# A new instruction order and another way of transposing half of the tiles, in a convolution and MLP kernel on one Trainium2 core

## The chip, the cores and the metric

The kernel runs on one core of a Trainium2 chip. The metric is device time in microseconds (us), lower is better. The core has five engines that run side by side, each in the order of its own queue: TensorE (PE: matmuls; its weight loads are listed as PEld), VectorE (DVE), ScalarE (ACT), GpSimd (POOL) and SyncE (SP, which here only issues DMAs). They wait for each other by semaphores. PE writes to PSUM, which DVE or ACT must empty ("evacuate") into SBUF. Sixteen DMA engines move data between HBM and SBUF, or within SBUF.

## The reference, cut to what matters

Sequence length S = 2048, width D = 640, hidden width F = 1728, all in bf16.

```python
x = A_q
# A: a gated long convolution
k_shift = 4-tap causal convolution of k, per channel (shift_k)
kv = k_shift * v
y  = irfft(rfft(kv, 2S) * rfft(ssm_k, 2S))[:S]      # convolution over the whole sequence
y  = y + kv * ssm_D
h  = x + layernorm(x) * y
# B: an MLP
a   = layernorm(h) @ w1 + b1
act = a * tanh(softplus(a))                          # Mish
h2  = h + act @ w2
```

## The kernel before, in words

The transform over the sequence is done by matmuls with tables, in stages. Channels go in five groups of 128, in three chunks (group 0; 1 and 2; 3 and 4). The names below are those of the operations in the order text; after the colon of each word there stands its engine (t PE, v DVE, a ACT, p POOL, d a DMA from SP).

- Loads: `d_n` (ssm_k), `d_k`, `d_v`, `d_g` (the table G), `d_x` (the input x in three parts).
- `k1pe` (line 543) transposes ssm_k on PE, `k1ev` evacuates, `dadd` (552) adds ssm_D to the first tap, so that the term kv * ssm_D needs no work of its own.
- `s1kpe`, `s1vpe` (469, 470): first stage of the forward transform of k and of kv, 20 groups each, of 16 weight loads and 16 matmuls. `ev` (374 on ACT, 376 on DVE) empties each group's PSUM bank, 1024 columns.
- `ktpe` (499), `ktsh` (508), `kspe` (522, 523): transposes of k and the 4-tap convolution; `kv` (528) multiplies by v on DVE.
- `s2kpe` (576), `s2vpe` (612): second stage with the table G. `s2kpe` needs every evacuation of `s1k`.
- `sw` (591, 592): DMAs that swap real and imaginary rows within SBUF. `p2` (631) and `p1` (628): the products of the two spectra, on DVE and POOL.
- `i1pe` (663, 664), then `i2pa`, `i2pb`, `i2pc` (734): the inverse transform; the last gives, for each of 16 tiles of 128 positions, a [128, 640] block y in PSUM. `d_t2m` loads its table; `d_w1` and `d_w2` load the MLP's weights.
- For each tile t: `y` evacuates, `lnx` (721, 723) is layernorm(x), `wb` (751; `wf`, 749, from PSUM for tiles 0 and 1) multiplies, `h` (755) adds x, `bn` and `pow` (760 to 765) take the statistics of h, `hc` (770) normalizes it into one of three buffers.
- `trpe` (778) transposes a normalized tile on PE, five blocks of 128x128, and `trev` (787) evacuates it into `lnhT`, where the tiles of a unit lie side by side: `lt_s` (315) has two buffers, in the memory of the table G, which is free by then.
- Units of 256, 256, 512, 512, 512 positions (tiles 0-1, 2-3, 4-7, 8-11, 12-15): `m1pe` (813, 809) is the product with w1, seven groups a unit; `hb` (822) applies bias and Mish on ACT; `m2pe` (839) is the product with w2, one a tile, 28 matmuls; `res` (849, 846) adds h and `d_out` (854, 861) stores. Tile 15 goes in three parts at the end.

PSUM is four buffers of 1024 columns, used in turn; PE can be at most four groups ahead of the evacuations.

The order of the work is written out: the text `ORDER` (from line 29 on) lists every operation with its engine. `_schedule` (143) walks it, gives each operation a start by the planner's costs, and picks the buffer of each ring that comes free first by those costs; the program is then emitted in the order of the starts. On each engine this is the order of the text; on SP, too. The planner has a rule for PE's instruction fetches (136, 161 to 169): instructions come in blocks, the next block is asked for as one is begun, it takes `_FETCH` 2.2 or, with transfers under way, `_SLOW` 5.0, and PE stands if it isn't there. [...]

## Time and profile before

| | |
|---|---|
| median of 3 runs | 233.67 us (232.84 to 280.52) |
| the profiled execution: time, span | 232.65 us, 230.9 us |
| instructions | 6501 |
| DMA traffic | 28.73 MB, mean 124 GB/s |
| granted TensorE clock, mean | 0.988 |
| ACT, evacuations L374 into uk (48) and uv (32) | 44.8 and 30.6 us |
| PE, second product L839 (462 matmuls) | 62.7 us |
| PE, first product L813 (318 records) | 57.9 us |

How to read it: the span is cut by windows (a stretch, then the busy time and, in brackets, the number of instructions of each engine, the clock that PE was granted, the share of the DMA engines and GB/s). The chain of work that ended last goes back from the last instruction to what released it; its rows give a start, a length and an engine with a line, and "issue" is time in which the engine waited for nothing that the profile shows. Groups give a line, an engine, an operation, what it wrote from what, the count, the busy time and the mean ns of one, and the idle time ahead of it. Lines are those of the kernel before.

### The profile page before, as it was taken

The page shows a single profiled execution, that of the slowest core. Times are in us where ns is not written, and L with a number is a line of the kernel's source. Part 1 is how long each engine was busy: PE and PEld are TensorE (multiplying, and loading weights), DVE is VectorE, ACT ScalarE, POOL GpSimd, SP SyncE. Part 2 cuts the span into 40 slices and gives each one's busy share as a digit, 9 for nine tenths or more (in the row PEclk, how much of TensorE's full clock was granted, in tenths as well). Part 3 has the DMA queues.
Part 4 walks back from the last instruction along what each step waited for, and adds up shares of the span by engine and source line. Part 5 has one row for each costly group of instructions (what it writes and reads, how often), then busy time and mean ns, then how long its engine had stood idle before and what let it go on. Part 6 is the DMA issues. An engine that isn't in the chain of part 4 may idle for free.

```text
span 230.9 us, 6501 instructions
## 1 busy us (share of the span) xinstructions
PE 219.5 (95%) x2842; PEld 169.1 (73%) x2849; DVE 139.2 (60%) x259; ACT 133.8 (58%) x184; POOL 70.7 (31%) x89
## 2 busy tenths in 40 slices
PE   7996999999789999999999999999999999999992
PEld 2986999899688999988877544777465445767772
DVE  0789899999997979888967735317921000112121
ACT  2576898999879999998827266311417608010000
POOL 0414850037770042764575891221000000000000
PEclk9999999999979999999999999999999999999998
DMA  6999992829962679500000100001100000001101
GB/s 189 420 382 398 429 404 76 231 61 282 317 161 82 230 285 385 166 0 4 0 3 0 57 1 3 0 28 60 57 0 31 0 0 0 31 0 57 61 28 57
DMA packets 19358, 28.73 MB, mean 124 GB/s; under 512 B 1409, under 2 KB 15746, under 8 KB 18946
## 3 DMA queue, kind: packets, MB, share of 16 engines
q1 hardware_dynamic: 19040, 28.17, 35.1%
q8 instruction: 22, 0.36, 0.6%
q10 hardware_dynamic: 194, 0.15, 0.2%
q14 instruction: 6, 0.05, 0.1%
q0 software_dynamic: 96, 0.00, 0.0%
HBM read 20.45 MB, written 2.62 MB: 100 GB/s over the span
## 4 chain that ended last, share of the span: by engine, by line
PE 79%; DVE 7%; ACT 7%; issue 4%; POOL 2%; DVEq 0%; ACTq 0%; POOLq 0%
PE ps L839 27%; PE ps L813 24%; ACT uv L374 4%; PE ps L734 4%; ACT uk L374 3%; PE ps L469 3%; PE ps L576 3%; PE ps L664 3%; PE ps L663 3%; PE ps L543 3%; PE ps L499 2%; PE ps L778 2%; PE ps L395 2%; DVE uv L376 2%; DVE ra L528 2%
## 5 line engine op out<-in xcount | busy, mean ns | idle before, releaser
L839 PE MATMUL ps<-rn,uv 128*128 128x320 bf16 (+2 forms) x462 | 62.7, 295 | 0.6 <-DVE xb L846 0.6
L822 ACT ACTIVATE uv<-ps,b1s 128x512 bf16<-128x512 f32 (+1 forms) x70 | 36.6, 605 | 42.1 <-PE ps L813 33.2
L813 PE MATMUL ps<-G 128*128 128x512 bf16 (+1 forms) x318 | 57.9, 336 | 0.4
L839 PEld LDWEIGHTS <-uv 128*128 128x128 bf16 x462 | 44.1, 98 | 17.0 <-issue 0.9
L813 PEld LDWEIGHTS <-G 128*128 128x128 bf16 x325 | 31.3, 98 | 23.4 <-issue 0.2
L374 ACT CAST uk<-ps 128x1024 bf16<-128x1024 f32 (+2 forms) x48 | 44.8, 1025 | 5.6 <-PE ps L470 3.4
L374 ACT CAST uv<-ps 128x1024 bf16<-128x1024 f32 x32 | 30.6, 1036 | 2.5 <-PE ps L470 2.0
L849 DVE TENSOR_TENSOR xb<-ps,xb 128x640 bf16<-128x640 f32 x5 | 4.1, 825 | 38.1 <-PE ps L839 38.1
L663 PE MATMUL ps<-a,uv 128*128 128x128 bf16 x160 | 18.5, 219 | 0.4 <-ACT uk L374 0.3
L663 PEld LDWEIGHTS <-uv 128*128 128x128 bf16 x160 | 17.9, 113 | 0.0
L376 DVE CAST uk<-ps 128x1024 bf16<-128x1024 f32 (+1 forms) x14 | 16.3, 1197 | 2.3 <-PE ps L664 1.2
L765 POOL TENSOR_TENSOR r<-ve,mhalf 128x1 f32<-128x1 f32 x16 | 9.1, 570 | 17.7 <-DVE ve L762 17.6
L612 PE MATMUL ps<-uv,G 128*128 128x64 bf16 (+1 forms) x384 | 13.7, 193 | 0.4 <-ACT uv L374 0.3
L612 PEld LDWEIGHTS <-G 128*128 128x128 bf16 x384 | 12.9, 101 | 1.0 <-issue 0.7
L374 ACT COPY G<-ps 128x640 bf16<-128x640 bf16 x8 | 5.5, 705 | 12.6 <-PE ps L778 12.6
L469 PE MATMUL ps<-cst,ra 128*64 128x128 bf16 x160 | 10.7, 220 | 2.2 <-issue 2.0
L528 DVE TENSOR_TENSOR ra<-ps,rb 128x1024 bf16<-128x1024 f32 x10 | 12.0, 1224 | 1.0 <-PE ps L523 1.0
L576 PE MATMUL ps<-uk,G 128*128 128x160 bf16 x128 | 11.7, 231 | 0.0
L469 PEld LDWEIGHTS <-ra 128*64 128x64 bf16 x160 | 9.3, 110 | 2.8 <-issue 2.4
L628 DVE TENSOR_TENSOR uv<-uv,uk 128x1024 bf16<-128x1024 bf16 x17 | 10.8, 686 | 0.1
L470 PE MATMUL ps<-cst,ra 128*64 128x128 bf16 x160 | 10.8, 221 | 0.0
L849 DVE TENSOR_TENSOR xa<-ps,xa 128x640 bf16<-128x640 f32 x6 | 4.9, 821 | 9.6 <-PE ps L839 9.6
(115 smaller groups left out, 377.0 us busy)
## 6 DMA issues: line engine op xcount, KB each, us to landing
G<-tab_g SPq DMA_DIRECT2D x8, 512.0 KB, 9.5
rn<-in_A_ssm_k_dram SPq DMA_DIRECT2D x5, 512.0 KB, 6.0
ra<-in_A_k_dram SPq DMA_DIRECT2D x4, 640.0 KB, 7.3
rb<-in_A_v_dram SPq DMA_DIRECT2D x2, 1280.0 KB, 12.4
G<-in_B_w_dram SPq DMA_DIRECT2D x5, 432.0 KB, 3.8
rn<-in_B_w_dram SPq DMA_DIRECT2D x1, 2080.0 KB
rn<-uk SPq DMA_DIRECT2D x4, 512.0 KB, 4.8
rb<-uk SPq DMA_DIRECT2D x4, 512.0 KB, 9.0
```

The lines of the kernel that those rows point to most:

```text
L374: nc.scalar.copy(o, i)
L376: nc.vector.tensor_copy(o, i)
L469: nc.tensor.matmul(ps[0:64, dgl, :], lhs, mc, start=True, stop=True)
L470: nc.tensor.matmul(ps[64:128, dgl, :], lhs, ms, start=True, stop=True)
L528: nc.vector.tensor_tensor(kv_w[:, m, :, 8 * h:8 * h + 8, :], rt.tile.rearrange("p (l t d) -> p d t l", l=4, t=8), raw_v[:, 8 * h:8 * h + 8 ...
L576: nc.tensor.matmul(ps[:, o:o + 160], g_v[:, f, :], KA[:, :, f, :], start=True, stop=True)
L612: nc.tensor.matmul(ps[:, fl * st:fl * st + n], g_v[:, f0 + fl, :], V[c.i][:, :, f0 + fl, :], start=True, stop=True)
L628: return eng.tensor_tensor(v, v, K[c.i][:, :, f0:f1, :], ALU.mult)
L663: nc.tensor.matmul(pz[:, dgl, :], V[c.i][:, dg // 4, :, dg % 4], a12[:, 0, :], start=True, stop=False)
L813: nc.tensor.matmul(ph[:, i * 512:i * 512 + w], w1[:, dc, fc * P:fc * P + P], lnhT_of(u)[:, dc, 0:w], start=(dc == 0), stop=(dc == NDC - 1))
L822: nc.scalar.activation(hb_of(u)[:, fc, 0:n], rt.tile[:, i * 512:i * 512 + n], ACT.Mish, bias=b1s[:, fc:fc + 1], scale=1.0)
L839: nc.tensor.matmul(po[:, a + a // 320 * 192:a + a // 320 * 192 + n], hb_of(u)[:, fc, o - x * w // 2:o - x * w // 2 + P], w2[:, fc + x, a:a ...
```

## The change

`MOVED = 3`: from unit 3 on, so for tiles 8 to 15, the normalized tile isn't transposed by PE. `hc` writes its 640 columns in another order (by 32 within each block of 128), a VectorE transpose (`dtr`) turns every 32x32 block of the tile, and DMAs within SBUF (`d_tr`, one for each pair of tiles, 16 DMAs of 32 partitions x 2 x 160 elements each, from SP's queue) carry the blocks to the partitions where they belong. The transposed pair lies in one of three new buffers in the memory of `uv0`, which the inverse transform has read by then. There are 40 transposes and 8 evacuations less, and 8 VectorE transposes and 64 DMAs more.

So that each DMA writes long rows, `lnhT` has another layout for all units: tile, then quarter of the tile (32 positions), then block of 128 channels, then position. `trev` of tiles 0 to 7 writes into it, and the first product reads its moving operand as 16 runs of 32 elements that are 160 elements apart.

And `ORDER` is a new text throughout; the planner and its rule for fetches are the same. On SP, `d_a12` goes from the head of the list to behind the `sw` of chunk 0, `d_x2` behind the first `sw` of chunk 2, and `sw0_1` and `sw1_1` stand next to each other; `d_small` (three small DMAs) stands earlier on POOL. Of `s2kev`, one of 22 is on DVE and 21 are on ACT (4 and 18 before). The two orders of PE in the first two stages:

```
before: ... k1pe3 s1kpe2_2 s1kpe2_0 s1kpe2_1 k1pe1 s1kpe2_3 s1kpe3_0 s1kpe0_1 s1kpe3_2 s1kpe3_3 s1kpe0_0 s1kpe1_3
  s1kpe0_3 k1pe4 s1kpe1_2 s1kpe1_1 s1kpe0_2 s1kpe4_0 s1kpe4_3 s1kpe4_2 s1kpe4_1 s1kpe3_1 s1kpe1_0 ktpe0_0 ...
  ... s1vpe3_0 s1vpe0_3 s1vpe3_1 s1vpe4_3 s1vpe4_0 s2vpe0_1 s1vpe4_1 s1vpe4_2 s1vpe3_3 s2vpe0_0 s2vpe2_7 ...
after:  ... k1pe1 s1kpe2_2 s1kpe2_3 s1kpe2_1 s1kpe2_0 k1pe4 s1kpe1_3 s1kpe0_1 s1kpe0_2 s1kpe1_1 k1pe3 s1kpe4_1
  s1kpe4_2 s1kpe0_0 s1kpe4_0 s1kpe1_0 s1kpe0_3 s1kpe3_1 s1kpe1_2 s1kpe3_0 s1kpe3_3 s1kpe3_2 s1kpe4_3 ktpe3_0 ...
  ... s1vpe4_1 s1vpe3_1 s1vpe3_3 s1vpe4_3 s1vpe0_1 s1vpe4_0 s1vpe3_0 s2vpe1_5 s2vpe0_1 s2vpe0_3 s2vpe2_6 ...
```

and of the second half:

```
after:  ... m2pe2 ... m1pe2_0 m2pe3 m2pe5 m2pe6 m1pe3_2 m2pe7 m1pe3_1 m1pe3_0 m1pe3_4 m1pe3_3 m1pe3_5 m1pe3_6 m2pe4 m2pe9 m2pe8
  m1pe4_1 m1pe4_6 m1pe4_5 m1pe4_4 m1pe4_2 m1pe4_0 m2pe11 m1pe4_3 m2pe10 m2ape15 m2pe13 m2pe12 m2pe14 m2bpe15 m2cpe15
DVE:    ... res5 res6 wb15 bn15 res7 hc14 dtr14 hc15 dtr15 res4 ...
SP:     ... d_w2 d_tr8 d_out1 d_out0 d_tr10 d_out2 d_out3 d_tr12 d_out5 d_out6 d_out7 d_tr14 d_out9 d_out4 ...
```

The diff outside of the order, cut:

```diff
+MOVED = 3
-    lt_s = [...rearrange("p (c s) -> p c s", c=NDC) for i in range(2)]
+    lt_s = [...rearrange("p (t r c j) -> p t r c j", t=4, r=4, c=NDC) for i in range(2)]
+    ht_s = [uv[0][:, i * 2 * D:(i + 1) * 2 * D].rearrange("p (t s) -> p t s", t=2) for i in range(3)]
...
             hc_rt.tile = slot(hc_rt, hc_s)
-            nc.vector.tensor_scalar(hc_rt.tile, xt(t2), mv2[:, t2, 0:1], r2[:, t2:t2 + 1], ALU.subtract, ALU.mult)
+            o, x = hc_rt.tile, xt(t2)
+            if U_OF[t2] >= MOVED:
+                o, x = o.rearrange("p (q c i) -> p c q i", q=4, i=32), x.rearrange("p (c q i) -> p c q i", q=4, i=32)
+            nc.vector.tensor_scalar(o, x, mv2[:, t2, 0:1], r2[:, t2:t2 + 1], ALU.subtract, ALU.mult)
...
+        if U_OF[t2] >= MOVED:
+            if t2 % 2 == 0:
+                ht_rt = _RT(R_HT)
+            def dtr(e, t2=t2, hc_rt=hc_rt, ht_rt=ht_rt):
...
+                nc.vector.transpose(ht_rt.tile[:, t2 % 2], hc_rt.tile)
...
+            def dmt(e, ht_rt=ht_rt, pair_of=pair_of):
+                dst = pair_of(2).rearrange("p t r c j -> p t r (c j)")
+                src = ht_rt.tile.rearrange("p t (q s) -> p t q s", q=4)
+                for r in range(4):
+                    for q in range(4):
+                        nc.sync.dma_start(dst[32 * q:32 * q + 32, :, r], src[32 * r:32 * r + 32, :, q])
...
-            ev(e, lnhT_of(u)[:, :, o:o + P], rtt.tile[:, 0:D].rearrange("p (c t) -> p c t", c=NDC))
+            ev(e, tile_of()[:, 0].rearrange("p r c j -> p c r j"), rtt.tile[:, 0:D].rearrange("p (c r j) -> p c r j", c=NDC, r=4))
...
-                        nc.tensor.matmul(ph[:, i * 512:i * 512 + w], w1[:, dc, fc * P:fc * P + P], lnhT_of(u)[:, dc, 0:w],
+                        nc.tensor.matmul(ph[:, i * 512:i * 512 + w], w1[:, dc, fc * P:fc * P + P], lnhT_of(u).rearrange("p t r c j -> p c (t r) j")[:, dc, 0:w // 32],
```

## The prediction

> **What bounds the kernel now.** I read the page's busy time first, then a table of windows, then the chain of work that ended last, and at the end single groups.

> ```profile
> PE 219.5 (95%) x2842; PEld 169.1 (73%) x2849; DVE 139.2 (60%) x259; ACT 133.8 (58%) x184; POOL 70.7 (31%) x89
> q8 instruction: 22, 0.36, 0.6%
> ```

> TensorE (PE) is busy for 95% of 230.9 us. The windows (length, then busy us and count on PE, PEld, DVE, ACT, POOL, then granted clock, DMA share, GB/s) show that this average covers two halves with different limits:

> ```profile
> 24.00:62.00 38.00, 37.65 (x855) 36.02 (x849) 35.96 (x38) 35.91 (x41) 15.98 (x15) 1.00 0.75 251
> ...
> 91.80:226.00 134.20, 133.62 (x1028) 90.29 (x1032) 59.64 (x149) 57.13 (x102) 37.75 (x45) 1.00 0.08 28
> ```

> From 91.8 to 226.0 PE lacks work for only 0.58 us, and VectorE (DVE), ScalarE (ACT) and the DMAs have much room. Whatever leaves PE there shortens the run by its own length, and nothing else can. From 24 to 62 three engines are full at once: PE 37.65, DVE 35.96, ACT 35.91 of 38. There an order of the same work can win only the little that all of them waste. The chain shows where PE stood for nothing that the profile names:

> ```profile
> 15.53 0.37 issue
> ...
> 21.59 1.06 issue
> ...
> 62.21 1.96 issue
> ```

> Beside them one wait that has a name, from the list of waits:

> ```profile
> PE ps L469 <- issue: 3.4, 3, 2.0
> ...
> PE ps L469 <- DVE rn L552: 0.8, 1, 0.8
> ```

> The same stretches as windows:

> ```profile
> 10.80:15.90 5.10, 4.68 (x130) 4.25 (x125) 4.80 (x5) 4.42 (x6) 1.33 (x3) 1.00 1.02 383
> 15.90:22.65 6.75, 4.88 (x130) 4.42 (x129) 5.84 (x8) 4.56 (x5) 2.23 (x2) 1.00 1.01 398
> 22.65:28.90 6.25, 6.25 (x129) 6.16 (x129) 5.29 (x9) 4.67 (x5) 5.50 (x5) 1.00 1.03 425
> 57.50:64.17 6.67, 4.54 (x146) 4.00 (x140) 6.61 (x8) 5.24 (x6) 4.75 (x4) 1.00 1.08 312
> 64.17:69.20 5.03, 4.87 (x126) 4.70 (x127) 5.03 (x9) 4.31 (x5) 3.74 (x6) 0.66 0.59 145
> ```

> Queue q8 moved 22 packets for 2842 + 2849 PE instructions, so one fetch brings about 259. Between the first two stalls PE ran 259 instructions, and in the window ahead of the third 286. I read the stalls as PE at the end of its block while the next is under way beside transfers (DMA share 1.01 and 1.08); a block then took 6.75 and 6.67 us. The third stall has a tail: from 64.17 to 69.20 the granted clock is 0.66, which loses 5.03 × 0.34 = 1.7 us.

> **The change, part by part.** All sums are against the profiled execution: span 230.9, time 232.65 us, so 1.75 lie around the span. The median of the three runs is 233.67, 0.4% above it.

> *PE's transposes of tiles 8 to 15 go.* They stand on the chain as pieces of L778:

> ```profile
> 148.42 0.56 PE ps L778 x10
> 148.98 3.80 PE ps L839 x28
> 152.78 0.28 PE ps L778 x5
> ...
> 156.87 0.28 PE ps L778 x5
> ...
> 167.67 0.56 PE ps L778 x10
> ...
> 174.19 0.28 PE ps L778 x5
> ...
> 176.63 0.28 PE ps L778 x5
> ```

> That is 40 transposes in 0.56 + 0.28 + 0.28 + 0.56 + 0.28 + 0.28 = 2.24 us, each with a product right behind it. I take **-2.24**. Their eight evacuations leave DVE and ACT (0.48 and 0.71 us each, next fence); off the path, nothing.

> *The first product reads its moving operand in runs of 32 columns.* The nearest rows are L576, whose moving operand is gathered in runs of 4, and L813 with its long rows:

> ```profile
> 27.29 0.42 PE ps L576 x6
> ...
> 129.53 10.74 PE ps L813 x49
> ```

> 0.42 / 6 / 160 = 0.44 ns per column against 10.74 / 49 / 512 = 0.43. Shorter runs cost PE nothing there, so I take 0.

> *Eight VectorE transposes, and a reordered hc.* No transpose on DVE is in this trace. The bounds for 128x640 are the plainest and the slowest rows of that size:

> ```profile
> L770 DVE TENSOR_SCALAR hc<-xb,mv,r 128x640 bf16<-128x640 bf16 x6 | 2.6, 440 | 0.0
> L376 DVE COPY G<-ps 128x640 bf16<-128x640 bf16 x8 | 3.9, 484 | 8.8 <-PE ps L778 8.5 <-ACT G L374 0.3
> L755 DVE TENSOR_TENSOR xa<-rb,xa 128x640 bf16<-128x640 bf16 x1 | 1.7, 1703 | 0.0
> L374 ACT COPY G<-ps 128x640 bf16<-128x640 bf16 x8 | 5.5, 705 | 12.6 <-PE ps L778 12.6
> ```

> So 0.44 to 1.70 us; I take 0.8, nearer the plain rows, as the operation also goes from SBUF to SBUF. Eight are 6.4 us (3.5 to 13.6), in a half where DVE is busy 59.64 of 134.20. Cost 0; the cover is the other work that PE has before units 3 and 4. hc at the 1.70 bound would add 10 us to DVE in the same room.

> *Sixty-four DMAs on SP's queue* (four pairs, 16 each), ahead of twelve of the result's DMAs. SP runs in order, and each DMA waits until the eighth before it has landed. SP's rows:

> ```profile
> L854 SPq DMA_DIRECT2D out_dram<-xa x6: 332/332/434, 157.8 to 224.3; - x6
> ...
> L591 SPq DMA_DIRECT2D xa<-uk x2: 1230/1232/1235, 39.7 to 50.9; - x2
> ...
> DMA to landing us min/median/max: 3.7/6.8/9.9
> ...
> DMA to landing us min/median/max: 1.8/1.8/2.7
> ...
> L849 DVE TENSOR_TENSOR xa<-ps,xa 128x640 bf16<-128x640 f32 x6 | 4.9, 821 | 9.6 <-PE ps L839 9.6
> ```

> The first landing line is L591's, the second L854's; the last row gives res7. One pair costs between 16 × 0.33 + 1.8 = 7.1 us and 16 × 1.23 + 9.9 = 29.6. I take about 12, nearer the low end, since these DMAs meet an idle fabric (share 0.08). Who waits: m1pe3 for pair 10, m1pe4 for pair 14. Pair 14 is tightest. After m2pe7 DVE does res7, two hc and two transposes, 0.82 + 0.88 + 1.6 = 3.3 us (2.6 to 5.1). Meanwhile PE has six groups of unit 3 (10 × 0.219 each, 13 us) and three second products (3.80 each, 11.4), so 24.4 in all. Pair 14 has 24.4 - 3.3 = 21 us, and needs 12: **0**. The results behind it on SP delay nobody; the last pair leaves over 50 us before the end.

> *The order of the first 92 us.* It moves what each engine waits for. In the new order, too, a block of PE instructions ends inside the k side's first stage, and another in the v side's, with sw2 and x2 on the queues. Each of these blocks is nearly all eight groups of 16 loads and 16 matmuls, 256 × 4.54 / 286 = 4.1 us of PE work by the fourth window. If a loaded fetch still takes 6.7 us, PE leaves those places when it did before. Bounds: all three stalls and the slow clock go, -(0.37 + 1.06 + 1.96 + 1.7) = -5.1; or the blocks stand for all that they are short of, 6.75 - 4.1 = 2.65 in place of 1.06 and of the 0.8 for L552's add, +0.8, and 6.67 - 4.1 = 2.6 in place of 1.96, +0.6. I take 0, since the two loaded windows agree at 6.7 whatever PE did inside them. [...]

> *Evacuations change engines.* Up to the last i1 evacuation ACT gets three more of s2k and otherwise as many as before; DVE loses three, and one product comes to it from POOL. The groups of ACT within 20 to 62:

> ```profile
> L374 ACT CAST uk<-ps 128x960 bf16<-128x960 f32 (+2 forms) x24 | 21.7, 958 | 2.6 <-PE ps L576 1.5 <-PE ps L470 0.8
> L374 ACT CAST uv<-ps 128x1024 bf16<-128x1024 f32 x20 | 18.9, 1022 | 0.3
> ```

> ACT gets 3 × 0.96 = 2.9 us more and has 38 - 35.91 = 2.1 free there: between 0 and +0.8 on the path, more if its waits stay. It starts on s2k sooner, as its share of the first stage ends with the last two groups; I take 0.

> *The rest of the queues.* The a12 load leaves SP's head (0.33 us of issue) and is needed only at i1; x2 goes behind the first half of sw2 and is read first by tile 10's statistics; the b1 loads stand earlier on POOL, which waits there for ktev in any case. All hidden: 0.

> Sum: 232.65 - 2.24 + 0 = **230.4**.

> **Rivals.**

> *A, the stalls go.* sw0_1 and sw1_1 now leave SP together after s2k instead of one by one, so the queues could be quieter when PE asks for the block it lacked at 62.21. For it: the window 22.65 to 28.90 shows a block of 258 with no stall. Against: sw2 still waits for the last kv, and it and x2 are 3 MB then. Price: the third stall with its slow clock, 1.96 + 1.7 = 3.7, so 226.7; at most 5.1, so 225.3.

> *B, ACT becomes the first half's limit.* For it: 35.91 of 38 busy, and 2.9 more. Against: it starts earlier. Price 0.8 to 2.9, so 231.2 to 233.3: not faster by more than 0.6%.

> *C, pair 14 is late (slower).* Place: PE before the first group of unit 4. It decides from (21 - 6.8) / 16 = 0.89 us a DMA. For it: L591 at 1.23. At the dear end 29.6 - 19.3 = 10.3 us late, so 240.7, 3.5% slower. Against: those issues stood in a full queue, and L854's take 0.33. [...]

> *D, no gain.* PE meets another wait where the transposes stood, a bank that DVE empties late: at most the 2.24 back, 232.65.

> **How the numbers follow.** Faster or slower than 2% (4.65 us, so under 228.0 or over 237.3) is about what a measurement of this kernel can tell from no change. My forecast, 228.8 to 231.6, has 0.45: the predicted time. A has 0.22, B and D 0.22 together, C 0.11. Faster is A (0.22); slower is C's larger part and a little for an order that strings several waits together (0.11 in all); same is the rest, 0.67. The range leaves out the best part of A and most of C: 226.0 to 235.0.

> **What would show it.** Right: L778 x40 on PE; PE without a gap from the first i2 to the end, and that stretch 2.2 us shorter; i1 ending near 92; stalls marked "issue" of 1 to 3 us near 21 and near 62. Transposes of 0.44 to 1.7 us on DVE; d_tr DMAs landing over 5 us before m1pe3 and m1pe4. Wrong: no stall near 62 and the clock at 1.00 there (A); ACT full with PE waiting for it between 45 and 92 (B); PE waiting for a DMA into G ahead of unit 3 or 4 (C); an L813 group over 2.2 us (strided reads).

## The result, and the profile after

| | before | after |
|---|---|---|
| median | 233.79 us (10 runs) | 232.08 us (10 runs, 231.31 to 232.92) |
| profiled execution: time, span | 232.65, 230.9 us | 232.92, 231.1 us |
| granted clock, mean | 0.988 | 0.985 |

The ratio is 0.9933, with a 95% interval of 0.9908 to 0.9958: 0.7% faster, where I forecast 230.4 us, 1.4% under the 233.67 shown. The 232.08 lies outside the 228.8 to 231.6 that I held likeliest, and inside the wide range. One run of 280.52 us, far from all others, is left out of the ratio. The two profiled executions alone would say that nothing was gained (+0.27 us). They are the first thing to learn from here: one profile of a kernel is one draw.

The busy lines and the stretches that answer to those of before, from the windows of the kernel after:

```profile
PE 218.8 (95%) x2809; PEld 168.5 (73%) x2809; DVE 141.7 (61%) x262; ACT 133.2 (58%) x183; POOL 63.8 (28%) x87
q8 instruction: 22, 0.36, 0.6%
```

```profile
24.00:62.00 38.00, 37.41 (x818) 36.10 (x814) 34.35 (x40) 35.77 (x41) 14.56 (x12) 0.97 0.68 226
...
92.99:227.06 134.07, 132.95 (x1010) 88.76 (x1008) 65.36 (x153) 54.11 (x98) 31.31 (x40) 1.00 0.16 51
102.25:227.06 124.81, 124.16 (x891) 81.07 (x891) 56.77 (x133) 46.88 (x86) 25.61 (x33) 1.00 0.11 31
```

The same two last stretches in the kernel before, from its first i2 to PE's end and from its first m1 to PE's end:

```profile
91.70:227.27 135.57, 134.48 (x1043) 90.99 (x1047) 60.16 (x150) 57.23 (x102) 37.85 (x45) 1.00 0.08 28
100.76:227.27 126.51, 125.52 (x920) 82.82 (x924) 52.56 (x131) 48.45 (x88) 31.38 (x37) 1.00 0.06 21
```

From the first m1 on, PE ends 126.51 - 124.81 = 1.70 us sooner. It does there one i2 tile more than before (three instead of two; 0.55 us by the chain of the kernel after, next fence), so that stretch became 2.25 shorter for the same work: the 2.24 of the forecast. (The order of the second half changed along with the transposes in every kernel that moves them, so no run prices the two apart.)

```profile
142.33 0.55 PE ps L737 x8
```

From the first i2 on only 1.50 is left. The pieces of the chain and the waits of the kernel after show why:

```profile
20.16 1.96 issue
...
66.84 2.39 issue
...
93.24 1.02 ACT uk L377
...
101.65 0.50 DVE G L379
102.15 0.14 issue
```

```profile
PE ps L737 <- ACT uk L377: 0.2, 1, 0.2
...
PE ps L849 <- DVE G L379: 0.2, 1, 0.2
```

Ahead of i2 PE now waits for the last i1 evacuation (L377, 1.02 us on ACT), and ahead of m1 for VectorE's evacuation of tile 1 (L379, 0.50 us), where the kernel before still had i2 work to do. From first i2 to first m1 it needs 102.25 - 92.99 = 9.26 us for 13 tiles, before 9.06 for 14: 0.55 + 0.20 = 0.75 us given away.

The end, on SP's queue, of the kernel before and then of the kernel after:

```profile
226.45 2.04 SPq L861 DMA_DIRECT2D out_dram<-xb  x3
```

```profile
225.62 0.42 SPq L890 DMA_DIRECT2D out_dram<-xa  x1
227.52 1.28 SPq L897 DMA_DIRECT2D out_dram<-xb  x3
```

In the order after, the second part of tile 15 stands ahead of the first on SP, so all three wait for the second's sum. From PE's end to the span's end it is 230.9 - 227.27 = 3.63 us before and 231.1 - 227.06 = 4.04 after. That is 0.41 more; as spans are given to 0.1 us, read 0.4 to 0.5.

### The profile page after: what moved, and what is told of

Read it like the earlier page. It is cut to its first block, busy times and chain, and to the rows that moved or that the text cites. A ratio compares the mean times of both kernels' runs of the same rounds, so it can differ in the third digit from the quotient of the medians.

```text
span 231.1 us, 6512 instructions
## 1 busy us (share of the span) xinstructions
PE 218.8 (95%) x2809; PEld 168.5 (73%) x2809; DVE 141.7 (61%) x262; ACT 133.2 (58%) x183; POOL 63.8 (28%) x87
## 4 chain that ended last, share of the span: by engine, by line
PE 81%; ACT 5%; DVE 4%; issue 4%; DVEq 0%; ACTq 0%
PE ps L875 26%; PE ps L849 25%; PE ps L667 4%; PE ps L666 4%; ACT uv L377 4%; PE ps L737 4%; PE ps L579 4%; PE ps L472 3%; PE ps L615 3%; PE ps L502 2%; ACT uk L377 2%; DVE uk L379 2%; PE ps L525 1%; DVE uv L379 1%; PE ps L473 1%
## 5 line engine op out<-in xcount | busy, mean ns | idle before, releaser
L849 PE MATMUL ps<-G 128*128 128x512 bf16 (+1 forms) x325 | 58.8, 337 | 0.2 <-DVE G L379 0.2
L377 ACT CAST uk<-ps 128x1024 bf16<-128x1024 f32 (+2 forms) x52 | 47.5, 1032 | 5.7 <-PE ps L473 3.5
L849 PEld LDWEIGHTS <-G 128*128 128x128 bf16 x325 | 31.2, 98 | 23.5 <-issue 0.7
L377 ACT CAST uv<-ps 128x1024 bf16<-128x1024 f32 x32 | 29.8, 1084 | 1.7 <-PE ps L615 1.7
L666 PE MATMUL ps<-a,uv 128*128 128x128 bf16 x160 | 19.6, 227 | 0.3 <-ACT uv L377 0.3
L615 PE MATMUL ps<-uv,G 128*128 128x64 bf16 (+1 forms) x384 | 12.6, 189 | 2.7 <-issue 2.4
L379 DVE CAST uk<-ps 128x1024 bf16<-128x1024 f32 (+1 forms) x10 | 12.1, 1217 | 4.8 <-PE ps L473 2.7
L615 PEld LDWEIGHTS <-G 128*128 128x128 bf16 x384 | 11.9, 98 | 3.1 <-issue 2.8
L631 DVE TENSOR_TENSOR uv<-uv,uk 128x1024 bf16<-128x1024 bf16 x18 | 11.4, 684 | 0.1
L472 PE MATMUL ps<-cst,ra 128*64 128x128 bf16 x160 | 10.2, 219 | 0.5 <-ACT uv L377 0.5
L737 PE MATMUL ps<-uk,ra 128*128 128x128 bf16 (+1 forms) x128 | 10.2, 232 | 0.3 <-ACT uk L377 0.2
L473 PE MATMUL ps<-cst,ra 128*64 128x128 bf16 x160 | 10.3, 221 | 0.0
L379 DVE CAST uv<-ps 128x1024 bf16<-128x1024 f32 x8 | 9.5, 1219 | 1.1 <-PE ps L473 0.7
## 6 DMA issues: line engine op xcount, KB each, us to landing
rn<-in_B_w_dram SPq DMA_DIRECT2D x1, 2080.0 KB, 15.5
```

What stands on the lines that cost most here:

```text
L377: nc.scalar.copy(o, i)
L379: nc.vector.tensor_copy(o, i)
L472: nc.tensor.matmul(ps[0:64, dgl, :], lhs, mc, start=True, stop=True)
L473: nc.tensor.matmul(ps[64:128, dgl, :], lhs, ms, start=True, stop=True)
L615: nc.tensor.matmul(ps[:, fl * st:fl * st + n], g_v[:, f0 + fl, :], V[c.i][:, :, f0 + fl, :], start=True, stop=True)
L666: nc.tensor.matmul(pz[:, dgl, :], V[c.i][:, dg // 4, :, dg % 4], a12[:, 0, :], start=True, stop=False)
```

## The experiments

All are compared with the kernel before on the same chip. The theory that I tested for the first half (F): PE stands at block boundaries of its instruction stream, for as long as the next block queues behind data, and a long stall brings a slow clock with it (in the first profile of before 0.66 over 5.03 us, behind the stall of 1.96). Rivals: ACT's added evacuations set the first half; the moved transposes cost something in the second.

**e1: the old first half, the new second half.** The order of before up to `i2pa6`, from there that of after, `MOVED = 3` as in after.

> The order of the kernel before up to i2pa6, then the order of the kernel after; tiles 8 to 15 transposed by VectorE and DMAs. Theory S (the second half alone makes the gain, and loses part of it to one more i2 tile that waits at its start and to the results' order on SP): PE from its first L628 group to its end shorter by 1.5 to 2.2 us than the 135.57 of before, the tail behind PE 0.36 longer, stalls at 15.5, 21.6 and 62.2 as in the kernel before; ratio to before 0.992 to 0.996 (-1.0 to -1.9 us). Rival (the moved transposes or their DMAs cost time somewhere): that stretch shorter by less than 1 us, ratio 0.997 to 1.000. Forecast as recorded: -2.24, ratio 0.990.

Measured: 234.96 us, ratio 1.0049 (1.0019 to 1.0080): neither. The seam that I made cost a large part of the difference from the -1.0 to -1.9 us that I had expected:

```profile
PE ps L737 <- DVE rb L752: 1.6, 1, 1.6
```

PE stood 1.6 us at its fourth i2 tile, tile 5, for a bank that VectorE emptied late, behind layernorm statistics that stood elsewhere in the first order. And the stall near 21.6 was 1.88 us, in the very order that had 1.06 in the first profile. First m1 to PE's end was 124.8, as in after; the time of e1 says nothing on the change.

**e2: the new first half, PE transposes.** After's order up to `i2pa0`, then before's, `MOVED = 5`, so that no tile is transposed by VectorE.

> The order of the kernel after up to i2pa0, then that of the kernel before; all tiles transposed by PE. Theory F (the first half is decided by where PE runs out of its instruction block while transfers fill the queues, and both orders have two or three such stalls): PE stalls of 1 to 2.5 us near 20 and 65; first half within 1 us of before; ratio 0.997 to 1.001. Rival B (ACT's three more evacuations limit the first half): PE waits for ACT between 25 and 62, ratio 1.003 to 1.006. Reading the two profiles as they stand: +1.3 us, ratio 1.0055.

Measured: 234.25 us, ratio 1.0029 (0.9994 to 1.0064). That is above what theory F allowed (1.001) and below rival B (1.003 to 1.006) by a hair. First m1 to PE's end is 126.5 as in before, so the 1.70 goes and comes with the transposes and the second half's order. No single wait of PE for ACT over 0.3 us stands in its first half, which speaks against ACT as the limit there. But this kernel has a seam too: at the start of i2 PE waits for the last i1 evacuation, ahead of which ACT does a layernorm (`lnx1`) from the old order.

```profile
PE ps L738 <- ACT uk L378: 0.5, 1, 0.5
```

From its first i2 product to its first m1 it needs 9.60 us for the 14 tiles that took 9.06 before. So 0.54 us of its loss is the seam's, and not the new first half's.

**e3: x2 late.** The 960 KB load of x2 moves from between the two halves of sw2 to behind t2m; `ln1_10` moves to just before `ln1_11`.

```diff
-s1vev3_1:v sw2_1:d s1vpe3_3:t s1vev3_3:a s1vpe4_3:t d_x2:d s1vev4_3:v ...
+s1vev3_1:v sw2_1:d s1vpe3_3:t s1vev3_3:a s1vpe4_3:t s1vev4_3:v ...
...
-... p1_2_6:v d_t2m:d d_w14:d ...
+... p1_2_6:v d_t2m:d d_x2:d d_w14:d ...
```

> The kernel after with the load of x2 issued behind t2m instead of ahead of the v side's sw2, and its first statistics later. Theory F: with 1.3 MB less on the queues the block that PE asks for near 63 us lands sooner, the 2.39 us stall at 66.8 shrinks to 1 us or less and the half clock near 70.6 to 74.0 goes; 1 to 4 us under the kernel after, ratio to before 0.976 to 0.989. Rival B (ACT limits the first half): the stall may move, but the last i1 group ends when it did, ratio as the kernel after, 0.991 to 0.996. Rival G (the sw2 halves alone fill the queues long enough): stall of 1.5 to 2.4 us stays, ratio 0.991 to 0.996, with PE rather than ACT as what is waited for.

Measured: 230.53 us, ratio 0.9872 (0.9827 to 0.9917). The stall at 66.84 of 2.39 us became:

```profile
66.34 1.29 issue
```

The clock was 1.00 from 7 us to PE's end. Theory F holds, though 1.29 us of the stall stayed where I had expected 1 or less; ACT's evacuations are the same here, and nothing of the first half depends on x2's data. (My move of `ln1_10` cost 0.5 us near 107, where VectorE came late to a normalization.)

**e4: the first part of tile 15 first.**

```diff
-... m2pe14:t res14:v d_out14:d resa15:v d_out8:d m2bpe15:t resb15:v d_outb15:d d_outa15:d ...
+... m2pe14:t res14:v d_out14:d resa15:v d_outa15:d d_out8:d m2bpe15:t resb15:v d_outb15:d ...
```

> The kernel after with the result of resa15 issued on SP directly behind resa15, ahead of the results of tile 8 and of resb15. Theory T: the span behind PE's end falls from 4.04 to about 3.6 us, everything else as in the kernel after: 0.3 to 0.4 us under it, ratio to before 0.990 to 0.993. Rival: the last result resc15 sets the end whatever stands ahead of it; tail 4.0 and no difference.

Measured: 231.56 us, ratio 0.9903 (0.9871 to 0.9936). PE ends at 226.21 of 229.8 us, a tail of 3.59, as before the change. That the order of the last results is worth about 0.45 us is shown by the profile; the times agree with it, though their intervals overlap.

**e5: 126 PE instructions more in front.**

```diff
-for _ in range(10):
-    nc.tensor.matmul(ps[:, 0:512], wz[:, 0:P], wz[:, P:D], start=True, stop=True)
+for _ in range(73):
+    nc.tensor.matmul(ps[:, 0:64], wz[:, 0:P], wz[:, P:P + 64], start=True, stop=True)
```

> The kernel after, with TensorE's ten warm-up matmuls of 512 columns replaced by 73 of 64 columns (nothing is computed from them): 126 more PE instructions (a load and a matmul each) in about the same time, ahead of all other work. Every later operation keeps its place in the order and stands 126 instructions later in the count. Theory F (PE stands at every 253rd instruction if the next block is not there): the stalls keep to the count and so leave their operations. In the kernel after they are inside s1kpe3_0 (instruction 710) and s2vpe0_0 (2734); here inside s1kpe1_0 and s2vpe2_6, 126 instructions of work earlier, again 1 to 2.5 us each; time within 1.5 us of the kernel after, ratio to before 0.987 to 1.000. Rival O (those two operations wait for data, or for a bank): the stalls stay inside s1kpe3_0 and s2vpe0_0, with the same lengths.

Measured: 232.66 us, ratio 0.9955 (0.9926 to 0.9983). The timeline of PE, first of the kernel after, then of e5 (the bracket is the idle time ahead of a row):

```profile
62.22 4.62 PE L615 MATMUL ps<-uv,G 128*128 128x64 bf16 x164
...
69.24 0.94 PE L615 MATMUL ps<-uv,G 128*128 128x32 bf16 x28 [2.39 <-issue]
```

```profile
61.30 2.83 PE L615 MATMUL ps<-uv,G 128*128 128x64 bf16 x101
67.15 3.09 PE L615 MATMUL ps<-uv,G 128*128 128x32 bf16 x84 [3.02 <-issue]
```

The first rows of both begin with the same operation. After 164 matmuls PE stands in the one, after 101 in the other: 63 fewer, the 63 that I added. The early stall went from `s1kpe3_0` back to `s1kpe1_0` as expected, but was only 0.58 us there, and a new one of 1.40 us came one block later. The late stall, 3.02 us, was longer than expected. No operation and no datum makes PE stand there; the count does. Counted in weight loads from the start, the late stall comes behind load 1375 in after, e2, e3, e4, e5, e7 and e9, and behind 1247 in before, e1, e6 and e8: 128 loads with their 128 matmuls, one block of 256, apart. (The 253 of my expectation is the figure that the planner in the kernel's text counts with; the traces show 256.) The shift didn't rid the kernel of the stalls: in the blocks that now ended in one, the DMA share was 1.01 to 1.03.

The traces also hold the packets that bring the blocks (queue q8, 16 KB each), and they name what PE stands for. At 28 ends of blocks, over the eleven traces, PE's loads pause for more than 0.4 us. Each time PE goes on 1.26 to 1.65 us after the next block's packet has landed, and nowhere is a block begun sooner than 1.23 us after its packet. At the late stall of the kernel after, the packet landed at 67.90 us and PE went on at 69.23. Counted from PE's start on the block before, that packet landed after 4.4 to 4.6 us in after, e2, e4 and e9, and after 3.4 in e3 and e7, which move x2: the 1.1 us by which the stall is shorter there. In the block that after begins at 75.81 us, with a DMA share of 0.01 over its 7.39 us, the next packet set out at 75.85 and landed at 76.75, after 0.95. With 1.23 us more that is the planner's 2.2; its 5.0 beside transfers stands against 4.8 (e7, late) to 7.6 us (e1, early) from a stalled block's start to the next's.

**e6: x2 late in the kernel before.** The same move of `d_x2` in before's order.

> The kernel before with the load of x2 issued behind t2m. Theory F: the stall at 62.21 (1.96 us, with a half clock behind it) shrinks to 1.3 us or less and the half clock mostly goes; 1 to 3.5 us under before, ratio 0.985 to 0.996. Rival G (sw2 alone fills the queues, x2 was not the cause in e3): stall of 1.5 to 2.4 stays, ratio 0.998 to 1.002.

Measured: 231.66 us, ratio 0.9908 (0.9884 to 0.9933); the third stall of 1.96 us with its slow clock became:

```profile
62.27 0.85 issue
```

So moving one word in the old order gives about as much as the whole change did.

**e7: x2 behind sw2, results in order.** After's order with `d_x2` behind `s2vpe0_0`, `d_outa15` as in e4.

> The kernel after with x2 issued only when s2vpe0_0 is done (near 69 us, behind the late fetch, so that tile 10's statistics keep their place) and with resa15's result ahead of resb15's. Theory F plus T: stall near 66 at 1.3 us or less and no half clock behind it, the 0.5 us that e3 lost between 99 and 108 us comes back, tail 3.6: 0.5 to 1 us under e3, ratio to before 0.981 to 0.987. Rival: x2 now meets the next fetch (asked for near 73) and PE stalls there for over 1 us; ratio 0.987 to 0.993.

Measured: 230.82 us, ratio 0.9856 (0.9818 to 0.9894): faster than both kernels. The added dependency held nothing back: SP issued x2 at 60.32, directly behind sw2's four DMAs, not near 69. Even that is enough, and the next block ends without a stall, so the rival is out:

```profile
60.32 3.46 SPq L677 DMA_DIRECT2D xb<-in_A_q_dram  x1
```

```profile
66.06 1.29 issue
```

```profile
66.10:69.52 3.42, 2.16 (x68) 2.17 (x69) 3.42 (x7) 3.33 (x4) 0.00 (x0) 1.00 0.49 191
69.52:72.93 3.41, 3.23 (x72) 3.13 (x70) 3.41 (x6) 3.41 (x5) 0.00 (x0) 1.00 0.00 0
...
99.19:223.99 124.80, 124.15 (x891) 81.10 (x891) 56.75 (x134) 46.93 (x86) 25.65 (x33) 1.00 0.11 30
```

The tail is 227.6 - 223.99 = 3.61 us. The ratio lies only 0.0016 under e3's, less than the 0.5 to 1 us expected and within both intervals; by the profile, the 0.5 us that e3 lost behind its first m1 is back.

**e8 and e9: both kernels once more.** No edit; each profiled once.

> The kernel before, unchanged, profiled once more. Theory W (the granted clock goes to half for 3.41 us when PE was idle for about 1.8 us or more of the 3.41 us stretch ahead of it, and these stretches lie on a grid that starts anywhere in a run): stalls at the same operations as in the first profile, near 21 and 62 us, of 0.5 to 2.5 us; a half clock behind a stall only where 1.7 to 2 us or more of it lie in one stretch of the grid; span 229.5 to 233. Rival: the stall lengths and half clocks belong to the order and come back as they were (0.37, 1.06, 1.96; one half clock behind the third); span 230.9 within 0.3.

> The kernel after, unchanged, profiled once more. Theory W: stalls inside s1kpe3_0 and s2vpe0_0 again, half clocks 0, 1 or 2 by where the grid falls; span 228.5 to 231.5, first m1 to PE's end 124.6 whatever the first half does. Rival: both half clocks come back, span 231.1 within 0.3.

Measured: before 235.58 us, span 233.8, against 232.65 and 230.9 in the first profile, and above the 233 that I had allowed; after 232.69, span 230.9. The second profile of before has these stalls:

```profile
21.84 1.61 issue
...
64.57 2.49 issue
```

From its first i2 on it is, to 0.01 us, the execution that I forecast from. The 2.9 us between two executions of one kernel lie wholly in the first half. The windows of the second profile of before, each stall's stretch and the one behind it, show the rest of the price:

```profile
20.03:23.44 3.41, 1.20 (x36) 1.09 (x37) 3.13 (x8) 2.61 (x3) 2.77 (x2) 1.00 1.03 405
23.44:26.86 3.42, 3.42 (x61) 3.24 (x61) 1.37 (x3) 1.93 (x2) 3.36 (x3) 0.50 1.06 440
64.40:67.82 3.42, 0.93 (x31) 0.67 (x27) 3.39 (x5) 0.88 (x2) 3.42 (x5) 1.00 1.17 291
67.82:71.23 3.41, 3.25 (x76) 3.17 (x73) 3.41 (x7) 3.25 (x4) 2.45 (x4) 0.50 0.45 107
```

In each trace all changes of the granted clock lie a multiple of 3.41 us apart, on a grid that starts anywhere (in after at 22.80, 26.21, 70.58 and 74.00 us, in before at 64.95 and 68.37). In every one of the eleven traces, where PE was busy 1.45 us or less of a stretch of the grid, the next ran at half clock (0.93 to 1.45 us at the stalls of before, after, e1, e8 and e9). The second profile of after had a stall as long as the first at the same early operation, but less of it in one stretch, and the clock stayed (its late stall was followed by half clock again):

```profile
18.93:22.34 3.41, 1.70 (x52) 1.43 (x50) 2.17 (x2) 2.75 (x4) 2.80 (x3) 1.00 1.03 409
22.34:25.76 3.42, 2.77 (x72) 2.60 (x72) 2.49 (x3) 1.93 (x2) 0.00 (x0) 1.00 1.05 420
```

At 1.58 to 1.70 busy both outcomes occur (half clock once, in e1; full clock in e3, e7 and e9). In before, 1.45 us of work in the stretch from 61.54 to 64.95 didn't save the clock of the next.

Not every stall differs from one execution to the next. In after's order the late one was 2.39 or 2.40 us, with a half clock behind it, in all four profiles that leave x2 and the count as they are (after, e2, e4, e9).

## Why the prediction was wrong, point by point

The side was right and the mechanism of the gain too; the size was not. Forecast 230.4, measured 232.08. What failed, in the terms of the sum:

- *The base.* The sum was made against 232.65, and the text set the median 0.4% above it aside. The median is now 233.79, so 1.14 of the 1.7 us lie here: that execution had one half clock and stalls of 1.06 and 1.96 us where e8 had two half clocks and 1.61 and 2.49. This doesn't touch the gain, only the predicted time.
- *PE's transposes, -2.24.* Right where they stood: 1.70 plus the added tile's 0.55. It came again in every kernel that has the edit, always with the new order of the second half: 124.8 from the first m1 to PE's end in after, e1, e4, e5, e7 and e9, 126.5 without it in before, e2, e6 and e8. e3, 0.5 longer, is the exception told above.
- *0 for the start of the second half* was mis-sized: 0.75. I had no step at all for which i2 tiles stand between the first half and m1. Rival D named such a loss ("PE meets another wait"), but put it where the transposes stood, not at m1's start.
- *"The results behind it on SP delay nobody"* was the step that failed on the queue: 0.4 to 0.5 us. I looked at what stands behind the 64 DMAs, and not at the order of the last three results, which the diff shows. e4 and e7 gave it back.
- *0 for the order of the first 92 us*, "since the two loaded windows agree at 6.7 whatever PE did inside them", was no reason. The second of those windows held 286 instructions, more than a block. Counted by whole blocks of 128 loads, from one block's first load to the next's, the early and the late stalled block took 6.7 and 6.2 us in the first profile of before, 7.3 and 6.7 in the second, 6.2 and 5.9 in both profiles of after, and 6.2 and 4.8 in e7 with x2 behind sw2. So it isn't fixed, and what else is on the queues moves it. The late block was quicker in after than in before, but PE had only 3.3 us of work in it (5.92 less a gap of 2.59 between loads) against 4.0, so it stood longer. What the new first half is worth by itself I can't settle: the medians leave 1.71 - 1.50 + 0.41, so about 0.6 us of gain for it; e2 points the other way, within its interval, and mostly by its seam. In the profiles the first i2 product starts at 91.75, 93.91 and 94.65 us with the old first half (before, e1, e8), and at 92.19, 92.20, 92.79 and 93.04 with the new (e4, e2, e9, after): too few and too far apart to tell.
- *Eight VectorE transposes.* Taken 0.8, measured 0.83 us, and hidden:

```profile
L788 DVE STREAM_TRANSPOSE uv<-hc 128x640 bf16<-128x640 bf16 x8 | 6.6, 832 | 0.2
```

- *Sixty-four DMAs.* Taken 12 us a pair, measured 10.2 to 10.7 of issue, and 1.8 (at most 3.8) from a DMA's issue to its landing. The timeline of SP, then the landing line of the group:

```profile
129.80 10.32 SPq L804 DMA_DIRECT2D G<-uv  x16
...
170.97 10.19 SPq L804 DMA_DIRECT2D G<-uv  x16
```

```profile
DMA to landing us min/median/max: 1.8/1.8/3.8
```

From the first issue to the last landing a pair took 11.4 to 13.5 us. Pair 14 has landed at 182.4, and unit 4's first m1 starts at 188.5: more than the 5 us of slack that the text asked for. Pair 10 landed at 154.5, 3.9 us ahead of unit 3's first m1 at 158.4: less than the text asked for, and enough. Rival C is out, though 0.595 us a DMA (the group's median) is nearly twice the 0.33 of the low end.

- *Strided reads of the first product.* 0, as taken: the mean of a matmul is 337 ns over the group (325 of them, L849), and was 336 (318, L813).
- *Rival B, ACT.* Out as the first half's limit: in 24 to 62 ACT is busy 35.77 us (35.91 before), and the waits of PE for ACT are 0.5 us or less in any place. What ACT does cost is at the end of i1, and is part of the 0.75 above.
- *Rival A, the stalls go.* The change didn't bring it, and its cause was wrong: not sw0 and sw1 issued together, but x2 out of the way of sw2 takes the stall down. The price was near: from e9 to e7, whose early stalls are alike, the profiled run falls from 232.69 to 229.35, 3.34 us, of which 0.4 to 0.5 are the tail; I had priced 3.7 for the whole stall, and 1.29 of it stays.

Still open: the first half's own worth, as said; and what makes one execution's block arrive 0.5 to 1 us later than another's in the same order. No kernel separated these.

## What to carry to other kernels

Before a sum is made, look for what in a profile is a draw: stalls without a name, and stretches of half clock, can belong to the execution as much as to the kernel (here before had one half clock in its first profile and two in its second; a second profile of the same kernel tells which), so forecast against the median and price the draw apart. Where PE stands for nothing that the profile names, count its instructions from one stall to the next; if the count is a block (here 128 loads with their 128 matmuls), look for a transfer that isn't needed yet in the queues at that time, and move that. An edit that takes work from a full engine is worth what it takes only if the order around it is still tight: read the starts of the stages and the last few entries of each queue too.
